# First expert weights loaded behind the last q and k tile, and steps 37 to 40 of an expert loop in conditional parts

## The chip, the cores and the metric

The kernel runs on one core of a Trainium2 chip. The metric is device time in microseconds (us), the median of several executions. The core has five engines with an instruction queue each: TensorE (PE: matmuls and transposes, PEld its weight loads), VectorE (DVE), ScalarE (ACT), GpSimd (POOL) and SyncE (SP). Here SP issues the loads of q, k, v and the weights, and POOL issues the writes of x_rows, the gathers and the scatters; all these transfers run on the same 16 DMA engines. Work passes from engine to engine through semaphores; each queue is served in order.

## The reference

Chunk attention first: q, k and v have the shape (8, 8, 576, 64) (batch, heads, sequence, head size), and a chunk of 64 positions attends only to itself.

```python
scores = scale * np.matmul(q_c, k_c.transpose(0, 1, 2, 4, 3))
scores = scores - np.max(scores, axis=-1, keepdims=True)
attn = np.exp(scores)
attn = attn / (np.sum(attn, axis=-1, keepdims=True) + 1e-09)
out = np.matmul(attn, v_c)
```

Its output, as x with 4608 rows (tokens) of 512, goes through a cosine router to one of 8 experts (w1 512 x 1024, w2 1024 x 512, all float32):

```python
logits = xn @ en.T / tau
expert_idx = np.argmax(logits, axis=1)
...
gate_w = probs[np.arange(N), expert_idx]
...
    h = np.maximum(x[mask] @ w1[e], 0.0)
    out[mask] = gate_w[mask, None] * (h @ w2[e])
```

## The kernel before, in words

There are three stages. The order of the work is written out by hand (`manual_schedule`, line 55): each engine executes its instructions in the order of the program.

**Attention** (lines 85 to 286). 36 tiles (`NT`) of 128 rows. The loop at line 259 is a software pipeline over t: in one iteration TensorE transposes the weights of tile t (`turn_a`), q and k of tile t + 3 (`turn_qk`, line 131), takes the logits of t - 2, the scores of t + 2, the transpose of x for t - 1 and the product with v of t (`values`, line 183). `load_qk(t + 7)` (line 266) puts the next q and k loads on SP's queue; four buffers each hold them, so a load waits until the tile four before it has been turned. `load_v` (line 119) issues eight loads for a batch, every 4.5 tiles. `values` writes the finished tile to a DRAM tensor, x_rows, from POOL's queue (line 210), from one of three x buffers. In the iteration t = 12 (`NT // 3`, line 278) `load_first(0)` (line 73) puts four weight transfers on SP's queue: w1 and w2 of expert 0 and of expert 7, 2 MB each, for the expert loop's first step.

**Seam** (lines 288 to 482). The buffers of attention are released, `late_p` takes part of the room, and `load_first(1)` (line 292) loads the same four weights into the second set. VectorE then works out the routing: the expert of each token, its rank, the gate, and the place of each token in blocks of 64 (`G`) of one expert. Two blocks make a step: side 0 takes the blocks from the front, side 1 from the back, and `mid` (line 382) is half of the number of blocks, rounded. There are tables for up to 40 steps (`NST` = 36 + 4): `src_row` and `dst_row` (which rows to gather and scatter; a row number out of range is left out), `gate_at`, `eblk` (expert of each side and step), `fresh` (1 where the expert differs from that of two steps before, whose buffer is used again).

**Expert loop** (lines 488 to 633). Step j gathers 128 rows (`gather`, four buffers ahead), transposes them (`turn_xb`), multiplies with w1 (`hidden`: 32 matmuls of 512 columns, the two sides on the two halves of the output partitions, then ReLU on VectorE and ScalarE), transposes h (`turn_h`), multiplies with w2 (`result`: 32 matmuls) and scatters the rows (line 598). The loop at line 619 is a software pipeline too: its body holds `hidden(j + 1)`, `turn_h(j)`, `turn_xb(j + 2)`, `result(j - 1)`, so that each copy out of PSUM has matmuls of another step beside it. `load_w1` and `load_w2` read expert and `fresh` into registers of SP (line 499) and issue a 2 MB transfer that takes place only where `fresh` is 1; it waits for the matmuls that read the buffer last. All 40 steps are issued.

Of the kernel before, what the change touches and what calls it, by code (L numbers as in the profile page):

```python
# [9 lines left out]
FP32 = mybir.dt.float32  # L10
BF16 = mybir.dt.bfloat16
I32 = mybir.dt.int32
AF = mybir.ActivationFunctionType
ALU = mybir.AluOpType
AX = mybir.AxisListType
PSUM = bass.MemoryType.PSUM
ENG = mybir.EngineType

P = 128
# [6 lines left out]
def kernel(  # L26
# [11 lines left out]
    nc = tc.nc  # L38
    B, H, S, Dh = q.shape
    E, D = moe_expert_emb.shape  # L40
    F = moe_w1.shape[2]
    N = B * S
    NPAIR = H // 2
    KD = D // P
    KF = F // P
    NT = N // P
    NCB = S // CH
    G = P // 2
    NST = NT + E // 2
# [4 lines left out]
    keep = ctx.enter_context(tc.tile_pool(name="keep", bufs=1))  # L54
    ctx.enter_context(tc.manual_schedule())


    w1_sb = [[keep.tile([P, KD, F], FP32, name=f"w1_{s}0")] for s in range(2)]
    w2_sb = [[keep.tile([P, KF, D], FP32, name=f"w2_{s}0")] for s in range(2)]
    w1_rows = moe_w1.rearrange("e (c p) f -> p (e c) f", p=P)  # L60
    w2_rows = moe_w2.rearrange("e (c p) d -> p (e c) d", p=P)
# [5 lines left out]
    gate_at = keep.tile([P, NST], FP32, name="gate_at")  # L67
    eblk = keep.tile([1, 2, NST], I32, name="eblk")
    fresh = keep.tile([1, 2, NST], I32, name="fresh")

    make_identity(nc, ident)

    def load_first(i):

        for s in range(2):
            e = (0, E - 1)[s]
            nc.sync.dma_start(out=w1_sb[s][i], in_=w1_rows[:, e * KD : e * KD + KD, :])
        for s in range(2):
            e = (0, E - 1)[s]
            nc.sync.dma_start(out=w2_sb[s][i], in_=w2_rows[:, e * KF : e * KF + KF, :])  # L80

# [2 lines left out]
    with (  # L86
# [18 lines left out]
        def load_qk(t):  # L105
            for src, nm in ((k, "kx"), (q, "qx")):
                x = qk_p.tile([P, H, Dh], FP32, tag=nm, name=nm)
                done = 0
                while done < P:
                    b, s = divmod(t * P + done, S)  # L110
                    n = min(P - done, S - s)
                    nc.sync.dma_start(  # L112
                        out=x[done : done + n],
                        in_=src[b, :, s : s + n, :].rearrange("h p d -> p h d"),
                    )
                    done += n
                qk_t[nm, t] = x.rearrange("p h d -> p (h d)")
# [13 lines left out]
        def turn_qk(t):  # L131
            for nm in ("kx", "qx"):
                a = qk_t.pop((nm, t))
                ps = ps_t.tile([P, NPAIR, P], FP32, tag="tr", name="tr")
                for i in range(NPAIR):
                    nc.tensor.transpose(ps[:, i], a[:, i * P : i * P + P], ident)  # L136
                x = wk.tile([P, NPAIR, P], FP32, tag=nm + "T", name=nm + "T")
                if nm == "kx":
                    nc.scalar.copy(x, ps)
                else:  # L140
                    nc.vector.tensor_copy(x, ps)  # L141
                qkT[nm, t] = x
# [31 lines left out]
        def turn_a(t):  # L174
            d = st[t]
            ps = ps_t.tile([P, NPAIR, P], FP32, tag="tr", name="tr")
            for i in range(NPAIR):
                nc.tensor.transpose(ps[:, i], d["a"][:, i].rearrange("p r k -> p (r k)"), ident)  # L178
            aT = wk.tile([P, NPAIR, P], FP32, tag="aT", name="aT")
            nc.scalar.copy(aT, ps)  # L180
            d["aT"] = aT
# [77 lines left out]
        for t in range(-3, NT + 2):  # L259

            if 0 <= t < NT:
                turn_a(t)
            if t + 3 < NT:
                turn_qk(t + 3)
                if t + 7 < NT:
                    load_qk(t + 7)
            if 0 <= t - 2:
                logits(t - 2)
            if 0 <= t + 2 < NT:
                scores(t + 2)  # L270
            if 0 <= t - 1 < NT:
                turn_x(t - 1)
            if 0 <= t < NT:
                values(t)
                b = (2 * t + 2) // NCB + 1
                if b not in v_t and b < B:
                    load_v(b)
                if t == NT // 3:
                    load_first(0)
            if 0 <= t + 2 < NT:  # L280
                weights(t + 2)
            if 0 <= t < NT:
                norm(t)
            if t == -2:
                set_up_experts()
        nc.vector.tensor_copy(lg, lg_ps)

    late_p = ctx.enter_context(tc.tile_pool(name="late", bufs=1))
    for s in range(2):
        w1_sb[s].append(late_p.tile([P, KD, F], FP32, name=f"w1_{s}1"))  # L290
        w2_sb[s].append(late_p.tile([P, KF, D], FP32, name=f"w2_{s}1"))
    load_first(1)

# [5 lines left out]
    with (  # L301
# [7 lines left out]
        io = sp.tile([P, P], FP32, name="io")  # L309
# [66 lines left out]
        mid = sp.tile([P, 1], FP32, name="mid")  # L376
# [28 lines left out]
        for i in range(2):  # L405
            nc.vector.tensor_scalar(
                fresh[:, i, 0:2], e_of[:, i, 0:2], float((0, E - 1)[i]), None, ALU.not_equal
            )
        nc.vector.tensor_tensor(
            fresh[:, :, 2:NST], e_of[:, :, 2:NST], e_of[:, :, 0 : NST - 2], ALU.not_equal  # L410
        )


# [12 lines left out]
            out=row, in0=blk, scalar=-float(G), in1=dest, op0=ALU.mult, op1=ALU.add  # L426
# [3 lines left out]
            out=row, in0=back, scalar=float(G), in1=row, op0=ALU.mult, op1=ALU.add  # L430
# [32 lines left out]
        for s in range(NT):  # L463
# [17 lines left out]
            out=dst_row, in0=tk, scalar=-1.0, in1=bad, op0=ALU.add, op1=ALU.add  # L481
# [7 lines left out]
    with (  # L489
# [5 lines left out]
    ):  # L495
        xin, mo = {}, {}

        def number(ap, top, engine):
            return nc.values_load(
                ap,  # L500
                engines=(engine,),
                min_val=0,
                max_val=top,
                skip_runtime_bounds_check_because="a count of comparisons, less than this",
            )
# [22 lines left out]
        def gather(j):  # L528
            t = bp.tile([P, D], FP32, tag="xin", name="xin", bufs=XBUF)
            nc.gpsimd.indirect_dma_start(  # L530
                out=t,
                out_offset=None,
                in_=x_rows,
                in_offset=bass.IndirectOffsetOnAxis(ap=src_row[:, j : j + 1], axis=0),
                bounds_check=N - 1,
                oob_is_err=False,
            )
            xin[j] = t
# [77 lines left out]
        hidden(0)  # L616
        load_w1(2)
        turn_xb(1)
        for j in range(NST + 1):
            if j + 1 < NST:  # L620
                hidden(j + 1)
                if j + 3 < NST:
                    load_w1(j + 3)
            if j < NST:
                turn_h(j)
            if j + 2 < NST:
                turn_xb(j + 2)
            if j > 0:
                result(j - 1)
                if j + 1 < NST:  # L630
                    load_w2(j + 1)
            if j + XBUF < NST:
                gather(j + XBUF)


# [26 lines left out]
```

## Time and profile before

| | |
|---|---|
| median of 3 runs (lowest to highest) | 862.99 us (862.68 to 863.69) |
| the profiled execution, its own time | 861.98 us |
| its span, first to last instruction | 860.2 us |
| mean granted TensorE clock | 0.956 |
| busy: PE / PEld / DVE / ACT / POOL | 794.9 / 392.8 / 223.8 / 187.4 / 105.2 us |
| moved by DMA | 142.58 MB, mean 166 GB/s |

A time of an engine in a row is its busy time; "L136" is line 136 of the kernel. A stretch A:B runs from A to B us after the span's start. The granted clock (PEclk) is a share of TensorE's full 2.4 GHz; 0.50 is its lower level, 1.2 GHz. A share of busy time is an average over stages with different limits, so each stage is read for itself.

### The profile page before, as it was taken

The page shows a single profiled execution, that of the slowest core. Times are in us where ns is not written, and L with a number is a line of the kernel's source. Part 1 is how long each engine was busy: PE and PEld are TensorE (multiplying, and loading weights), DVE is VectorE, ACT ScalarE, POOL GpSimd, SP SyncE. Part 2 cuts the span into 40 slices and gives each one's busy share as a digit, 9 for nine tenths or more (in the row PEclk, how much of TensorE's full clock was granted, in tenths as well). Part 3 has the DMA queues.
Part 4 walks back from the last instruction along what each step waited for, and adds up shares of the span by engine and source line. Part 5 has one row for each costly group of instructions (what it writes and reads, how often), then busy time and mean ns, then how long its engine had stood idle before and what let it go on. Part 6 is the DMA issues. An engine that isn't in the chain of part 4 may idle for free.

```text
span 860.2 us, 15300 instructions
## 1 busy us (share of the span) xinstructions
PE 794.9 (92%) x6287; PEld 392.8 (46%) x6287; DVE 223.8 (26%) x436; ACT 187.4 (22%) x346; POOL 105.2 (12%) x136
## 2 busy tenths in 40 slices
PE   5899299980789999999999999999999999999997
PEld 4799288970733333333333333333333334333332
DVE  3677256758511101011010110101101011010110
ACT  4577246761000111011110111101111111111011
POOL 1111001110110011010110101001010010100101
PEclk9999789995589999999999999999999999999999
DMA  9999999929110001045763157875214252147560
GB/s 208 238 246 274 376 229 245 251 98 348 61 47 22 26 34 41 25 146 192 263 231 123 50 188 272 330 307 196 74 37 151 107 197 74 38 154 298 200 234 1
DMA packets 153670, 142.58 MB, mean 166 GB/s; under 512 B 115702, under 2 KB 115702, under 8 KB 153600
## 3 DMA queue, kind: packets, MB, share of 16 engines
q1 hardware_dynamic: 144256, 112.21, 42.7%
q0 software_dynamic: 9344, 29.39, 9.6%
q8 instruction: 50, 0.82, 0.4%
q14 instruction: 20, 0.16, 0.1%
HBM read 391.14 MB, written 19.92 MB: 478 GB/s over the span
## 4 chain that ended last, share of the span: by engine, by line
issue 69%; PE 15%; POOL 7%; DMA 4%; DVE 3%; POOLq 0%; ACT 0%; SPq 0%; DVEq 0%; ACTq 0%
POOL xin L530 5%; PE tr L136 3%; PE lg_ps L229 2%; PE sc L152 2%; DMA kx<-in_k_dram 2%; POOL out_dram L598 2%; PE inv L466 2%; PE pv L192 2%; PE tr L178 2%; PE tr L221 2%; DMA qx<-in_q_dram 2%; POOL x_rows L210 1%; DMA x_rows<-x 0%; SPq L112 0%; POOLq L530 0%
## 5 line engine op out<-in xcount | busy, mean ns | idle before, releaser
L556 PE MATMUL h_ps<-w,xbT 128*64 128x512 f32 x1280 | 283.2, 595 | 2.4 <-DVE xbT L546 2.4
L589 PE MATMUL y_ps<-w,hT 128*64 128x512 f32 x1280 | 283.3, 595 | 0.0
L556 PEld LDWEIGHTS h_ps<-w,xbT 128*64 128x64 f32 x1280 | 92.0, 138 | 185.5 <-issue 182.3
L589 PEld LDWEIGHTS y_ps<-w,hT 128*64 128x64 f32 x1280 | 88.4, 137 | 167.0 <-issue 167.0
L567 DVE TENSOR_SCALAR h<-h_ps 128x512 f32<-128x512 f32 x40 | 27.7, 692 | 376.5 <-PE h_ps L556 376.5
L598 POOL DMA_INDIRECT out_dram<-y,dst_row x40 | 40.6, 1014 | 531.2 <-ACT y L597 515.8
L597 ACT ACTIVATE y<-y_ps,gate_at 128x512 f32<-128x512 f32 x40 | 27.5, 688 | 272.6 <-PE y_ps L589 272.6
L565 ACT ACTIVATE h<-h_ps 128x512 f32<-128x512 f32 x40 | 24.0, 600 | 284.0 <-PE h_ps L556 284.0
L581 DVE COPY hT<-ht_ps 128x512 f32<-128x512 f32 x40 | 27.7, 692 | 136.6 <-PE ht_ps L577 136.6
L577 PEld LDWEIGHTS ht_ps<-ident,h 128*128 128x128 f32 x320 | 34.3, 140 | 32.5 <-issue 32.5
L530 POOL DMA_INDIRECT xin<-x_rows,src_row x40 | 41.0, 1024 | 49.5 <-DVE dst_row L480 37.6
L136 PE MATMUL tr<-ident,kx 128*128 128x128 f32 x144 | 24.1, 294 | 22.3 <-DMA kx<-in_k_dram 22.3
L577 PE MATMUL ht_ps<-ident,h 128*128 128x128 f32 x320 | 43.7, 280 | 0.0
L210 POOL DMA_DIRECT2D x_rows<-x x36 | 19.6, 544 | 168.7 <-DVE x L203 140.3
L229 PEld LDWEIGHTS lg_ps<-enT,xT 128*128 128x128 f32 x288 | 35.9, 196 | 1.0 <-ACT xT L223 0.9
L229 PE MATMUL lg_ps<-enT,xT 128*128 128x8 f32 x288 | 35.5, 250 | 0.7 <-ACT xT L223 0.7
L141 DVE COPY qxT<-tr 128x512 f32<-128x512 f32 x36 | 24.9, 692 | 36.1 <-PE tr L136 34.3
L160 DVE TENSOR_REDUCE mx<-sc 128x8 f32<-128x512 f32 x36 | 24.9, 692 | 26.9 <-PE sc L152 26.9
L546 DVE COPY xbT<-x_ps 128x512 f32<-128x512 f32 x40 | 27.7, 692 | 13.8 <-PE x_ps L544 9.3
L544 PE MATMUL x_ps<-ident,xin 128*128 128x128 f32 x160 | 24.5, 277 | 5.2 <-DMA xin<-x_rows,src_row 5.2
L466 PE MATMUL inv<-rr,oh 128*128 128x80 f32 x72 | 15.7, 422 | 14.6 <-DVE oh L465 14.6
L136 PEld LDWEIGHTS tr<-ident,kx 128*128 128x128 f32 x144 | 18.1, 151 | 23.7 <-issue 15.2
(118 smaller groups left out, 503.2 us busy)
## 6 DMA issues: line engine op xcount, KB each, us to landing
w<-in_moe_w_dram SPq DMA_DIRECT2D x168, 2048.0 KB
v<-in_v_dram SPq DMA_DIRECT2D x64, 144.0 KB
x_rows<-x POOLq DMA_DIRECT2D x36, 256.0 KB, 3.7
kx<-in_k_dram SPq DMA_DIRECT2D x32, 256.0 KB
qx<-in_q_dram SPq DMA_DIRECT2D x32, 256.0 KB
kx<-in_k_dram SPq DMA_DIRECT2D x8, 128.0 KB
qx<-in_q_dram SPq DMA_DIRECT2D x8, 128.0 KB
xin<-x_rows,src_row POOLq DMA_INDIRECT x40, 3.6
```

The source lines that it names most:

```text
L136: nc.tensor.transpose(ps[:, i], a[:, i * P : i * P + P], ident)
L210: nc.gpsimd.dma_start(out=x_rows[P * t : P * t + P, :], in_=x)
L229: nc.tensor.matmul(lg_ps[:, t], lhsT=d["xT"][:, c], rhs=enT[:, c], start=(c == 0), stop=(c == KD - 1),)
L466: nc.tensor.matmul(inv.rearrange("p t k -> p (t k)"), lhsT=oh, rhs=rr[:, s].rearrange("p t k -> p (t k)"), start=(s == 0), stop=(s == NT - 1),
L530: nc.gpsimd.indirect_dma_start(out=t, out_offset=None, in_=x_rows, in_offset=bass.IndirectOffsetOnAxis(ap=src_row[:, j : j + 1], axis=0), ...
L546: nc.vector.tensor_copy(xT, ps)
L556: nc.tensor.matmul(ps[G * s : G * s + G], lhsT=d["xT"][:, c, G * s : G * s + G], rhs=w1_sb[s][j % 2][:, c, fh * 512 : fh * 512 + 512], sta ...
L567: nc.vector.tensor_scalar(dst, ps, 0.0, None, ALU.max)
L577: nc.tensor.transpose(ps[:, c], d["h"][:, f0 : f0 + P], ident)
L581: nc.vector.tensor_copy(hT[:, 4 * g : 4 * g + 4], ps)
L589: nc.tensor.matmul(ps[G * s : G * s + G], lhsT=d["hT"][:, c, G * s : G * s + G], rhs=w2_sb[s][j % 2][:, c], start=(c == 0), stop=(c == KF ...
L598: ins = nc.gpsimd.indirect_dma_start(out=out, out_offset=bass.IndirectOffsetOnAxis(ap=dst_row[:, j : j + 1], axis=0), in_=y, in_offset=Non ...
```

## The change

Six of the eight tiles of the first weights (all but the second set of w2) now lie in the pool that lives through the whole kernel. `load_first` loads one matrix of both sides. In the iteration t = 29, where the last `load_qk` has been issued in the iteration before, SP issues six weight transfers (w1 of both sets, w2 of the first); w2 of the second set is still loaded after attention, into `late_p`, which is now half as large. `load_first(0)` at t = 12 is gone.

In the seam, `used` marks the steps below `mid`, `n_steps` keeps `mid` as an integer, and `fresh` is multiplied by `used`.

The expert loop's pipeline runs over 36 steps (`LEAST`). Then all five engines read `n_steps` into a register, and `more(36)` holds step 37 whole, one part after the other, under a condition; inside it is the condition for step 38, and so on to step 40.

```diff
-    w1_sb = [[keep.tile([P, KD, F], FP32, name=f"w1_{s}0")] for s in range(2)]
+    w1_sb = [[keep.tile([P, KD, F], FP32, name=f"w1_{s}{i}") for i in range(2)] for s in range(2)]
...
-    def load_first(i):
+    def load_first(buf, rows, n, i):
 
         for s in range(2):
             e = (0, E - 1)[s]
-            nc.sync.dma_start(out=w1_sb[s][i], in_=w1_rows[:, e * KD : e * KD + KD, :])
-        for s in range(2):
-            e = (0, E - 1)[s]
-            nc.sync.dma_start(out=w2_sb[s][i], in_=w2_rows[:, e * KF : e * KF + KF, :])
+            nc.sync.dma_start(out=buf[s][i], in_=rows[:, e * n : e * n + n, :])
...
                 if t + 7 < NT:
                     load_qk(t + 7)
+                elif t + 7 == NT:
+                    load_first(w1_sb, w1_rows, KD, 0)
+                    load_first(w1_sb, w1_rows, KD, 1)
+                    load_first(w2_sb, w2_rows, KF, 0)
...
-                if t == NT // 3:
-                    load_first(0)
...
     for s in range(2):
-        w1_sb[s].append(late_p.tile([P, KD, F], FP32, name=f"w1_{s}1"))
         w2_sb[s].append(late_p.tile([P, KF, D], FP32, name=f"w2_{s}1"))
-    load_first(1)
+    load_first(w2_sb, w2_rows, KF, 1)
...
+        used = sp.tile([1, NST], I32, name="used")
+        nc.vector.tensor_scalar(used, io[0:1, 0:NST], mid[0:1], None, ALU.is_lt)
+        nc.vector.tensor_copy(n_steps, mid[0:1])
         nc.vector.tensor_tensor(
             fresh[:, :, 2:NST], e_of[:, :, 2:NST], e_of[:, :, 0 : NST - 2], ALU.not_equal
         )
+        nc.vector.tensor_tensor(
+            fresh, fresh, used.unsqueeze(1).to_broadcast([1, 2, NST]), ALU.mult
+        )
...
-        for j in range(NST + 1):
-            if j + 1 < NST:
+
+        LEAST = NT
+        for j in range(LEAST + 1):
+            if j + 1 < LEAST:
                 hidden(j + 1)
                 if j + 3 < NST:
                     load_w1(j + 3)
-            if j < NST:
+            if j < LEAST:
                 turn_h(j)
-            if j + 2 < NST:
+            if j + 2 < LEAST:
                 turn_xb(j + 2)
             if j > 0:
                 result(j - 1)
...
+        steps = number(n_steps, NST, ENG.PE, ENG.DVE, ENG.Activation, ENG.Pool, ENG.SP)
+
+        def more(j):
+            with tc.If(steps > j):
+                turn_xb(j)
+                hidden(j)
+                if j + 2 < NST:
+                    load_w1(j + 2)
+                turn_h(j)
+                result(j)
+                if j + 2 < NST:
+                    load_w2(j + 2)
+                if j + 1 < NST:
+                    more(j + 1)
+
+        more(LEAST)
```

## Rows read from the trace of the kernel before

**Rows 1.** Busy time by stretch: engines, then PEclk, DMA share, GB/s.
```profile
30.00:77.00 47.00, 47.00 (x987) 43.45 (x987) 34.97 (x70) 32.43 (x68) 6.52 (x14) 1.00 1.04 247
91.00:107.00 16.00, 1.92 (x49) 1.40 (x40) 2.35 (x5) 2.41 (x5) 0.54 (x1) 0.62 1.03 375
194.00:237.00 43.00, 16.85 (x79) 16.14 (x79) 29.61 (x95) 3.24 (x4) 3.93 (x7) 0.50 0.54 204
249.00:825.00 576.00, 575.22 (x2854) 217.80 (x2852) 78.86 (x114) 69.84 (x112) 72.44 (x71) 1.00 0.41 146
```

**Rows 2.** Waits of SP's queue, 25 to 77 us: total, times, longest.
```profile
SPq L112 <- PE tr L136: 9.3, 11, 1.8
```

**Rows 3.** Timeline of POOL in attention: start, duration, instruction, idle time before.
```profile
39.96 0.54 POOL L210 DMA_DIRECT2D x_rows<-x  x1 [3.60 <-DVE x L203]
...
89.08 0.54 POOL L210 DMA_DIRECT2D x_rows<-x  x1 [3.55 <-DVE x L203]
94.06 0.54 POOL L210 DMA_DIRECT2D x_rows<-x  x1 [4.44 <-DVE x L203]
115.87 0.54 POOL L210 DMA_DIRECT2D x_rows<-x  x1 [21.27 <-DMA qx<-in_q_dram]
...
182.12 0.54 POOL L210 DMA_DIRECT2D x_rows<-x  x1 [3.55 <-DVE x L203]
```

**Rows 4.** Timeline of SP's issues in attention.
```profile
77.51 2.01 SPq L77 DMA_DIRECT2D w<-in_moe_w_dram  x2
...
90.85 4.26 SPq L112 DMA_DIRECT2D kx<-in_k_dram  x1
...
169.95 0.81 SPq L112 DMA_DIRECT2D qx<-in_q_dram  x1
```

**Rows 5.** Timeline of the seam.
```profile
194.60 0.20 POOL masks.py:65 MEMSET sltb<- 128x128 bf16 x1 [2.06 <-DMA x_rows<-x]
...
204.41 0.22 DVE L409 TENSOR_TENSOR fresh<-e_of 1x76 int32<-1x76 f32 x1
```

**Rows 6.** Timeline of POOL at the end of the expert loop.
```profile
780.87 1.02 POOL L598 DMA_INDIRECT out_dram<-y,dst_row  x1 [13.00 <-ACT y L597]
...
826.90 1.01 POOL L598 DMA_INDIRECT out_dram<-y,dst_row  x1 [14.33 <-ACT y L597]
...
856.74 0.98 POOL L598 DMA_INDIRECT out_dram<-y,dst_row  x1 [5.93 <-ACT y L597]
```

**Rows 7.** The scatters of line 598, 812 to 828 us.
```profile
DMA to landing us min/median/max: 7.0/7.0/7.0
```

**Rows 8.** The scatters of line 598, 850 to 861 us.
```profile
DMA to landing us min/median/max: 2.1/2.1/2.1
```

**Rows 9.** The writes of line 210 (x_rows), 78 to 96 us.
```profile
DMA to landing us min/median/max: 5.5/5.9/6.3
```

**Rows 10.** The writes of line 210 (x_rows), 165 to 195 us.
```profile
DMA to landing us min/median/max: 2.3/3.1/3.7
```

**Rows 11.** Timeline of TensorE at the start of the expert loop.
```profile
238.51 8.68 PE L556 MATMUL h_ps<-w,xbT 128*64 128x512 f32 x32 [0.79 <-DVE xbT L546]
247.13 0.66 PE L544 MATMUL x_ps<-ident,xin 128*128 128x128 f32 x4
248.57 3.65 PE L556 MATMUL h_ps<-w,xbT 128*64 128x512 f32 x16 [0.78 <-DVE xbT L546]
```

**Rows 12.** Timeline of the kernel's last microseconds.
```profile
840.70 1.09 PE L577 MATMUL ht_ps<-ident,h 128*128 128x128 f32 x8
...
841.45 0.69 DVE L581 COPY hT<-ht_ps 128x512 f32<-128x512 f32 x1 [7.35 <-PE ht_ps L577]
...
841.73 13.95 PE L589 MATMUL y_ps<-w,hT 128*64 128x512 f32 x64
```

**Rows 13.** SP's register loads at line 499: duration ns min/median/max, first and last start.
```profile
L499 SPq TENSOR_LOAD <-eblk x80: 262/268/474, 204.4 to 802.2; - x80
```

**Rows 14.** The queue that fetches instructions: packets, MB, share of 16 engines.
```profile
q8 instruction: 50, 0.82, 0.4%
```

More of the change, by code (lines that the diff above doesn't have):

```diff
@@ L69 @@
     fresh = keep.tile([1, 2, NST], I32, name="fresh")
+    n_steps = keep.tile([1, 1], I32, name="n_steps")
     make_identity(nc, ident)
-    def load_first(i):
+    def load_first(buf, rows, n, i):
         for s in range(2):
             e = (0, E - 1)[s]
-            nc.sync.dma_start(out=w1_sb[s][i], in_=w1_rows[:, e * KD : e * KD + KD, :])
-        for s in range(2):
-            e = (0, E - 1)[s]
-            nc.sync.dma_start(out=w2_sb[s][i], in_=w2_rows[:, e * KF : e * KF + KF, :])
+            nc.sync.dma_start(out=buf[s][i], in_=rows[:, e * n : e * n + n, :])
     VW = 72
@@ L496, with number @@
         xin, mo = {}, {}
-        def number(ap, top, engine):
+        def number(ap, top, *engines):
             return nc.values_load(
                 ap,
-                engines=(engine,),
+                engines=engines,
                 min_val=0,
```

## The prediction

> **What bounds the kernel now.** I read the busy times by stretch first, then the issues of POOL and SP in order of time through attention, then the timelines of the seam, of the expert loop and of its end, and last the landings. They show three stages, and a bound for each.
>
> In attention TensorE is busy for all of 30 to 77 us while the DMA engines move 247 GB/s [rows 1], and in nearly that stretch it is SP that waits for TensorE to free q and k buffers, 11 times at one line alone [rows 2]: TensorE sets the pace, one tile of 128 rows in (89.08 - 39.96) / 12 = 4.09 us [rows 3]. Then the four weight transfers that `load_first(0)` puts on SP's queue (issued from 77.51 us) hold the queue; the next k tile is not issued before 90.85 us [rows 4]. In 91 to 107 us TensorE does 1.92 us of work at a granted clock of 0.62, which mixes 2.4 and 1.2 GHz, while DMA moves 375 GB/s [rows 1]: 8.39 MB of weights stand ahead of 256 KB that TensorE needs. The tile written out at 94.06 is followed by the next at 115.87 [rows 3].
>
> The seam (the routing between attention and the experts) is one long chain on VectorE with transfers beside it; its first work waits for the last write of x_rows [rows 5].
>
> In the expert loop TensorE is busy 575.22 of 576 us at the full clock, 2.4 GHz [rows 1]. A step costs (826.90 - 780.87) / 3 = 15.34 us by the scatters [rows 6]. All 40 steps are paid, whether or not they hold tokens. How many do is fixed by the inputs: the reference's argmax gives the experts 832, 359, 183, 448, 512, 1023, 576 and 675 tokens, in blocks of 64 that is 13, 6, 3, 7, 8, 16, 9 and 11, together 73, two to a step: 37 steps (j = 0 to 36). The trace agrees: the scatter at 826.90 is that of j = 36 (the one at 856.74 is j = 39, two lie between) and took 7.0 us to land [rows 6, 7], the last ones landed in 2.1 us [rows 8].
>
> **The change, attention.** Tiles 16 to 33 (first and last of 17 intervals: 89.08 and 182.12) took 93.04 us, and 17 x 4.09 is 69.6 [rows 3]. The loss around the weights is thus 23.4 us, close to 8.39 MB at 375 GB/s = 22.4 us. Moved behind tile 36's q and k, the weights have no q, k or v load behind them on SP (v for the last batch is issued earlier). Six transfers move, 12.6 MB, about 34 us at that rate: from some 147 us (the last q tile's issue, 169.95 [rows 4], less 23.4) to about 185 us with the x_rows writes among them. I take the whole 23.4 as gained, and give back 0.9: the tile at 94.06 came 4.98 us after the one before instead of 4.09, the loads already on the way having shared the engines with the weights, and the last tile will meet that. Bounds: 0, as its loads are ahead in the queue, and 2 us, if its 512 KB go at half of 375 GB/s beside weights.
>
> **The seam.** The remaining `load_first` (4.2 MB, 11 us) starts when attention's buffers are released and queues behind the flood; no matmul of the loop begins before 238.51 [rows 11], 44 us after that release [rows 5], so it costs nothing. The x_rows writes on POOL's queue do pay. In the present flood four landed in 5.5 to 6.3 us, median 5.9 [rows 9]; the last ones of attention, with little beside them, took as little as 2.3 [rows 10]. Three x buffers cover 6.3 us at a tile each 3.3 us or more. But the last write is what POOL's first seam work waits for [rows 5], and it now falls into the flood (attention ends near 170 us): 5.9 - 2.3 = **+3.6**. Bounds: 0, if the flood thins out or the buffers reused are others, and 4.0. Three small VectorE operations are added (`used`, `n_steps`, the product with `fresh`); the one next to them took 0.22 us [rows 5]: **+0.6**, bounds 0.3 and 0.7. SP's loads of `fresh` come later by that much, which nobody feels, as both first weight sets are there.
>
> **The loop.** Steps 37 to 40 leave the pipelined loop: -4 x 15.34 = **-61.4**. Step 37 then runs by itself in the order turn, hidden, turn, result. A turn of x with its copy exposed shows at the loop's start: 247.13 to 248.57, 1.44 us [rows 11]. `result` is 13.95 / 2 = 6.98 us, and `hidden`, as many matmuls of the same size, too; the turn of h is 0.75 us until the copy begins (840.70 to 841.45) plus 0.69 us of copy, 1.5 with the hand-over [rows 12]. Together **+16.9**. Its second copy hides behind the first half of `result`. Its weights: j = 36 has a fresh expert on one side; the w2 load is issued after `result` of j = 34, and between that and its use lie `result` of j = 35 and the first three of these, 16.9 us for 2.1 MB (5.6 us at 375 GB/s), so that is covered; w1 has longer. Masking `fresh` removes six later loads, whose cover was the same TensorE work: nothing. On SP, the loads of j = 38 wait inside the conditional part for step 37's matmuls, with only its own branch behind them. POOL's gathers stay ahead of the conditional part.
>
> **The end and the branches.** The last scatter now carries rows. It took 2.1 us empty [rows 8], 7.0 beside a weight load [rows 7]; nearest is a quiet write of the same 256 KB, 3.1 [rows 10]: **+1.0**, bounds 0 and 4.9. Reading `n_steps` on five engines and two branches on each: no row shows a branch. A register load took 0.26 to 0.47 us [rows 13]. At the entry I take **+0.5** on TensorE; below 0, since its sequencer may run ahead of the array; above 6.2, if the part begins with all engines joined: from TensorE's last matmul to the end of the span are 860.2 - 855.68 = 4.5 us, and after such a gap `hidden` may run as after the seam, 8.68 instead of 6.98 [rows 11, 12]. A gain is excluded, as only instructions are added. At the exit every engine jumps over three bodies: **+1.1**, what one 16 KB packet of the instruction queue takes (0.4% of 16 x 860.2 us over 50 packets [rows 14]); below 0, hidden behind the scatter's landing; above 6.9, three jumps one after another at the shortest landing of a write, 2.3 for rows written [rows 10].
>
> The Trainium skill's Runtime: NRT & Kernel Launch, section Instruction fetch mechanics, says that a taken branch to code outside the two pages held forces a fetch before execution goes on. No run here shows that yet. By it alone the exit would be one fetch or more, by a free branch 0.
>
> **The sum.** -23.4 + 0.9 + 3.6 + 0.6 - 61.4 + 16.9 + 1.0 + 0.5 + 1.1 = -60.2 against the profiled execution's 861.98 us (span 860.2): 801.8. The median of the runs, 862.99, is 1.0 above that execution; so 802.8, **803**.
>
> **Rivals.**
> First, dear branches: three fetches in a row at the exit, 6.9 instead of 1.1, make 803 + 5.8 = 809; a join at the entry, 6.2 instead of 0.5, makes 809 too, and both 815. For it: the conditional part can't mix with work outside it, and five engines read the count each for itself. Against it: only two branches lie on the path, and the exit has a landing to hide behind. The fetches are what the cited page of the Trainium skill would lead one to expect.
>
> Second, attention stays short of data. A tile needs 1.05 MB in 4.09 us, 256 GB/s, and 30 to 77 us shows 247 [rows 1]; if the loads fall behind by that 3.5% over the 20 later tiles, 82 us, that gives 3 us back: 806. Against it: SP waits for buffers in that very stretch [rows 2], so loading is ahead.
>
> Third, the change doesn't skip. If the count read were 40, three more lone steps with their entries would run, 3 x (16.9 + 0.5) = 52: 855. Against it: the count of 37 above.
>
> Fourth, on the other side: the clock. In the seam TensorE is granted 1.2 GHz (0.50 [rows 1]), and it has 2.4 GHz back within the first `hidden` (8.68 against 6.98 us [rows 11, 12]). If that came later by more than the 60 us saved, the kernel would be slower: four steps at half speed cost 61. At eight steps it would be 803 + 8 x 15.34 = 926. Against it: the same work stands there as before.
>
> **How the numbers follow.** The forecast has 0.64 and holds 796 to 807: its low end leaves out the 0.9, the 3.6, the 1.0 and the 1.6 of branches (803 - 7.1 = 796), its high end adds 4 us of the bounds. Dear branches have 0.20 (0.10 the fetches, 0.07 the join, 0.03 both), attention short of data 0.12, no skip 0.03, the clock 0.01. The range is 796 to 812: it takes in the second rival and the cases with one dear branch, and leaves out two of them together, no skip and the clock. A measurement of this kernel tells 0.2%, 1.7 us, from no change. All cases but the last are faster by more than that; I leave 0.01 for no change, since several terms could fail at once.
>
> **What would show it.** In the profile of the changed kernel: x_rows written every 4.09 us from the fourth tile to the 33rd without a gap; weight issues only after the last q tile; landings near 6 us at attention's end and the seam's first POOL work released by one; 37 scatters, the last with TensorE gaps under 1 us before its `hidden` and its `result`. Gaps of 4 us and more there, or a long stretch after the last matmul, would mean dear branches; waits for kx after 90 us, the second rival; 40 scatters, the third; a loop step over 15.34 us, the fourth. Outside 796 to 812 a term of the sum is wrong.

## The result and the profile after

The changed kernel takes 820.47 us (818.87 to 823.09, 4 runs); the kernel before, run beside it, 863.34 us (862.68 to 864.77). The ratio is 0.9504, 95% interval 0.9476 to 0.9533. The change saves 43 us where 60 were forecast, and 820 is outside the range of 796 to 812. The profiled execution took 820.02 us, its span 818.2 us against 860.2: -42.0.

Attention first. This is POOL's timeline of the changed kernel (start, duration, instruction, idle time before), which answers to [rows 3, 5].

```profile
43.67 0.54 POOL L208 DMA_DIRECT2D x_rows<-x  x1 [3.61 <-DVE x L201]
...
117.44 0.54 POOL L208 DMA_DIRECT2D x_rows<-x  x1 [3.55 <-DVE x L201]
127.56 0.54 POOL L208 DMA_DIRECT2D x_rows<-x  x1 [9.57 <-DVE x L201]
133.21 0.54 POOL L208 DMA_DIRECT2D x_rows<-x  x1 [4.94 <-DVE x L201]
...
179.90 0.54 POOL L208 DMA_DIRECT2D x_rows<-x  x1 [2.75 <-DVE x L201]
186.94 0.20 POOL masks.py:65 MEMSET sltb<- 128x128 bf16 x1 [6.50 <-DMA w<-in_moe_w_dram]
...
225.88 1.10 POOL L535 DMA_INDIRECT xin<-x_rows,src_row  x1 [38.07 <-DVE dst_row L485]
```

The 21.8 us gap behind the tile of 94.06 [rows 3] is gone. But the fourth tile comes at 43.67 instead of 39.96, 3.7 late before any moved instruction is reached, and there is a new gap: 117.44 to 133.21 holds two intervals of 10.12 and 5.65 us instead of 4.09, 7.6 lost. So the last write moves from 192.00 to 179.90, 12.1 us, where 22.5 were forecast. From it to the seam's first POOL work it is 7.04 us, before 194.60 - 192.00 = 2.60; the profile names a weight transfer as releaser, but the last write of x_rows took 6.3 us to land, which is about the same moment (the landings of the last six writes):

```profile
DMA to landing us min/median/max: 5.9/6.3/7.5
```

The windows of the changed kernel, the columns as in [rows 1] (the last two numbers are the DMA share and GB/s, ahead of them the granted clock):

```profile
30.00:77.00 47.00, 47.00 (x980) 42.90 (x983) 34.23 (x67) 30.93 (x65) 6.29 (x13) 0.97 1.02 233
91.00:107.00 16.00, 16.00 (x332) 14.64 (x332) 11.79 (x24) 11.13 (x25) 2.32 (x5) 1.00 1.09 236
242.00:780.00 538.00, 537.22 (x2664) 203.09 (x2662) 72.63 (x105) 65.41 (x105) 69.15 (x68) 1.00 0.37 131
```

TensorE now works through 91 to 107 us, and in the expert loop it is busy 537.22 of 538 us at the full clock. But the same loads arrive at 233 GB/s in 30 to 77 us, where it was 247. That stretch alone tells little: f1 below has 234 GB/s there and is faster.

Last, the end of the changed kernel, by TensorE's timeline [rows 12] and then POOL's [rows 6]:

```profile
773.20 13.95 PE L594 MATMUL y_ps<-w,hT 128*64 128x512 f32 x64
787.09 0.66 PE L549 MATMUL x_ps<-ident,xin 128*128 128x128 f32 x4
788.53 7.09 PE L561 MATMUL h_ps<-w,xbT 128*64 128x512 f32 x32 [0.78 <-DVE xbT L551]
795.54 1.45 PE L582 MATMUL ht_ps<-ident,h 128*128 128x128 f32 x8
797.04 7.09 PE L594 MATMUL y_ps<-w,hT 128*64 128x512 f32 x32
```

```profile
805.22 1.00 POOL L603 DMA_INDIRECT out_dram<-y,dst_row  x1 [15.96 <-ACTq L645]
```

The lone step 37 takes 804.13 - 787.09 = 17.0 us, the parts as reckoned, and it begins right behind the step before: TensorE loses nothing at the entry to the conditional part. But from the last matmul (804.13) to the end of the span are 14.07 us, where it was 4.5. The stretches add up (us of the profiled executions):

| stretch | forecast | measured |
|---|---|---|
| last write of x_rows | -22.5 | -12.1 |
| from it to the seam's first work | +3.6 | +4.4 |
| seam to the first gather (38.47, now 38.94) | +0.6 | +0.5 |
| first gather to last matmul (622.61, now 578.25) | -44.0 | -44.4 |
| last matmul to the end | +2.1 | +9.55 |
| sum | -60.2 | -42.0 |

Two terms are wrong, attention by 10.4 us and the end by 7.45.

### The profile page after: what moved, and what is told of

It is laid out like the page before. It is cut to its first block, busy times and chain, and to the rows that moved or that the text cites. A ratio compares the mean times of both kernels' runs of the same rounds, so it can differ in the third digit from the quotient of the medians.

```text
span 818.2 us, 14809 instructions
## 1 busy us (share of the span) xinstructions
PE 749.4 (92%) x6059; PEld 375.7 (46%) x6059; DVE 217.9 (27%) x430; ACT 181.6 (22%) x337; POOL 101.9 (12%) x133
## 2 busy tenths in 40 slices
DMA packets 148726, 129.99 MB, mean 159 GB/s; under 512 B 115366, under 2 KB 115366, under 8 KB 148656
## 3 DMA queue, kind: packets, MB, share of 16 engines
q1 hardware_dynamic: 139552, 99.63, 42.5%
## 4 chain that ended last, share of the span: by engine, by line
PE 86%; DMA 6%; DVE 3%; issue 2%; SPq 1%; ACT 1%; POOL 0%; POOLq 0%
PE y_ps L594 31%; PE h_ps L561 30%; PE ht_ps L582 5%; PE tr L134 4%; DMA w<-in_moe_w_dram 3%; PE lg_ps L227 3%; PE sc L150 3%; PE pv L190 2%; PE tr L176 2%; PE tr L219 2%; DMA qx<-in_q_dram 2%; PE x_ps L549 2%; PE inv L471 2%; DMA xin<-x_rows,src_row 0%; SPq L78 0%
## 5 line engine op out<-in xcount | busy, mean ns | idle before, releaser
L561 PE MATMUL h_ps<-w,xbT 128*64 128x512 f32 x1184 | 262.2, 595 | 3.1 <-DVE xbT L551 3.1
L594 PE MATMUL y_ps<-w,hT 128*64 128x512 f32 x1184 | 262.0, 595 | 0.0
L561 PEld LDWEIGHTS h_ps<-w,xbT 128*64 128x64 f32 x1184 | 85.0, 138 | 172.3 <-issue 168.0
L594 PEld LDWEIGHTS y_ps<-w,hT 128*64 128x64 f32 x1184 | 81.8, 137 | 154.6 <-issue 154.3
L572 DVE TENSOR_SCALAR h<-h_ps 128x512 f32<-128x512 f32 x37 | 25.6, 692 | 341.0 <-PE h_ps L561 341.0
L603 POOL DMA_INDIRECT out_dram<-y,dst_row x37 | 37.5, 1013 | 490.1 <-ACT y L602 474.1
L602 ACT ACTIVATE y<-y_ps,gate_at 128x512 f32<-128x512 f32 x37 | 25.4, 688 | 251.8 <-PE y_ps L594 245.2
L582 PEld LDWEIGHTS ht_ps<-ident,h 128*128 128x128 f32 x296 | 31.7, 141 | 30.4 <-issue 30.0
L582 PE MATMUL ht_ps<-ident,h 128*128 128x128 f32 x296 | 40.7, 280 | 0.1
L134 PE MATMUL tr<-ident,kx 128*128 128x128 f32 x144 | 24.6, 299 | 10.8 <-DMA kx<-in_k_dram 10.7
L213 ACT ACTIVATE junk<-x 128x512 f32<-128x512 f32 x36 | 22.7, 630 | 21.9 <-DVE x L201 21.9
```

Of the source, the lines that this page charges most:

```text
L561: nc.tensor.matmul(ps[G * s : G * s + G], lhsT=d["xT"][:, c, G * s : G * s + G], rhs=w1_sb[s][j % 2][:, c, fh * 512 : fh * 512 + 512], sta ...
L572: nc.vector.tensor_scalar(dst, ps, 0.0, None, ALU.max)
L582: nc.tensor.transpose(ps[:, c], d["h"][:, f0 : f0 + P], ident)
L594: nc.tensor.matmul(ps[G * s : G * s + G], lhsT=d["hT"][:, c, G * s : G * s + G], rhs=w2_sb[s][j % 2][:, c], start=(c == 0), stop=(c == KF ...
L603: ins = nc.gpsimd.indirect_dma_start(out=out, out_offset=bass.IndirectOffsetOnAxis(ap=dst_row[:, j : j + 1], axis=0), in_=y, in_offset=Non ...
```

## The experiments

The theories, by letter where an expectation uses one. **A**: attention falls short of data, since a tile needs 256 GB/s and gets less (the second rival of the prediction). **B**: the end is long because of the conditional parts. **C**, formed after the first four runs: the 4-byte tile `n_steps` moves all later buffers by 32 bytes, and that slows the loads. **D**, also formed then: POOL needs the time at the end behind a scatter that writes rows, with or without conditional parts. **E**: the seam's late start comes from the weight flood alone. The kernel before took 865.72 us beside e1 to e4, 866.0 beside f1 to f4 and 865.95 beside g1 to g4.

**e1_again.** The changed kernel, no edit.

> The changed kernel, unaltered, profiled once more. Theory A (the loads of q, k and v together with the x_rows writes need 256 GB/s and the DMA engines give about 237): TensorE again waits for q and k in mid-attention, 5 to 10 us in all after the third tile, and the last x_rows write is issued at 176 to 183 us. Rival (the wait of 6 us before the tile written at 127.56 was a chance of that execution): no wait over 2 us after the third tile, last write at 168 to 173 us. The end after the last matmul again takes 13 to 15 us by every theory.

One run took 825.26 us (span 823.5). The last x_rows write came at 184.63, just outside the 176 to 183 of A, and the end was 14 us again. Attention's stalls vary by some 5 us between executions; the rest repeats.

**e2_weights_only.** The kernel before with the part of the change in `w1_sb`, `load_first`, its calls and `late_p`; no `n_steps`, no conditional parts.

> The weight loads moved, the loop as before with all 40 steps. Theory A: attention 10 to 14 us shorter than before, the seam's start 4 us later after the last x_rows write: 863.3 - 12.1 + 4.4 = 855.6 us (853 to 859). The prediction's reckoning (the whole 23.4 us are gained) would give 863.3 - 22.5 + 3.6 = 844.4 us.

846.89 us (845.99 to 849.78), ratio 0.9788 (0.9758 to 0.9817). That is nearer to the prediction's reckoning than to A. POOL's timeline of this run:

```profile
37.82 0.54 POOL L207 DMA_DIRECT2D x_rows<-x  x1 [3.61 <-DVE x L200]
...
95.13 0.54 POOL L207 DMA_DIRECT2D x_rows<-x  x1 [3.55 <-DVE x L200]
103.28 0.54 POOL L207 DMA_DIRECT2D x_rows<-x  x1 [7.21 <-DVE x L200]
109.11 0.54 POOL L207 DMA_DIRECT2D x_rows<-x  x1 [5.28 <-DVE x L200]
...
172.19 0.54 POOL L207 DMA_DIRECT2D x_rows<-x  x1 [2.75 <-DVE x L200]
179.09 0.20 POOL masks.py:65 MEMSET sltb<- 128x128 bf16 x1 [6.36 <-DMA w<-in_moe_w_dram]
```

Moving the weights alone brings the last write to 172.19, 19.8 us earlier. The gap is there, as A says, but the late start of the fourth tile is not. Something in the other half of the change slows attention.

**e3_cond_only.** The changed kernel without e2's part: weights loaded as before, conditional parts kept.

> The conditional parts alone, the weights loaded as before. Theory B (the end pays some 9.5 us more because POOL has to make up for skipped scatters): 863.3 - 44.4 + 0.6 + 9.5 = 829 us (827 to 831), 14 us from the last matmul to the end of the span. If the end were cheap without the moved weights: 820 us.

844.05 us (842.91 to 845.58), ratio 0.9746 (0.972 to 0.9771): 15 us more than expected, and not at the end (843.3 - 829.2 = 14.1 us behind the last matmul, as in the changed kernel) but in attention, where this edit moves no instruction. The last write comes at 207.19 instead of 192.00. Already the first 20 us show it (window of this run):

```profile
0.00:20.00 20.00, 10.06 (x97) 7.93 (x98) 5.47 (x12) 7.05 (x10) 2.28 (x10) 1.00 1.21 190
```

190 GB/s, where the kernel before moves 209 with the same instructions. What differs there is where the buffers lie. `n_steps` stands in the pool `keep` behind `fresh`; it takes 32 bytes of each partition, and all later buffers follow it. In the memory plan of the built programs (not of a trace) kx begins at byte 84992 before (332 x 256), at 85024 in e3 (32 more) and at 117792 in the changed kernel (460 x 256 + 32, behind two more w1 tiles). This is C.

**e4_static37.** The changed kernel with 37 steps in the loop and no conditional parts (37 is what these inputs need).

```diff
-        LEAST = NT
+        LEAST = NT + 1
...
-        steps = number(n_steps, NST, ENG.PE, ENG.DVE, ENG.Activation, ENG.Pool, ENG.SP)
...
-        more(LEAST)
```

> The changed kernel with a plain loop of 37 steps and no conditional part (right for these inputs only, since the count is not asked). It gives the whole price of the branches: theory B 820.5 - 9.1 at the end - 1.6 for the lone step = 809.8 us (808 to 812), 5 us from the last matmul to the end. If the long end came from somewhere else (the last scatter with rows, or the gathers of steps that do not run), it stays at 13 to 15 us and the time is 819 us.

824.93 us (820.27 to 829.44), ratio 0.9545 (0.9511 to 0.9579), its interval overlaps that of the changed kernel. Its last matmuls in TensorE's timeline, and POOL's DRAIN at the end (by line: count, duration ns min/median/max, first and last start):

```profile
799.10 7.08 PE L594 MATMUL y_ps<-w,hT 128*64 128x512 f32 x30 [2.68 <-DMA w<-in_moe_w_dram]
```

```profile
L664 POOLq DRAIN  x3: 51/99/10707, 807.0 to 818.2; - x3
```

The end is 818.5 - 806.18 = 12.3 us long without any branch, so B can hold for 14.07 - 12.3 = 1.75 us only. Most of it is one DRAIN of POOL, 10.7 us. In the plain loop TensorE also waits 2.68 us for the last w2, which the lone step hides.

**f1_pad.** The changed kernel, `n_steps` in a tile of 256 bytes, so that later buffers move by 256 instead of 32.

```diff
-    n_steps = keep.tile([1, 1], I32, name="n_steps")
+    n_steps = keep.tile([1, 64], I32, name="n_steps")[:, 0:1]
```

> The changed kernel with n_steps given 256 bytes a partition in place of 4, so that the buffers behind it (q, k, v, x and those of the loop) start where they start in the kernel before, at a multiple of 256 bytes, and not 32 bytes behind one. Theory C (the 32 bytes cost the 256-byte packets of q and k their speed): the first 20 us move 205 to 215 GB/s as in the kernel before and not 188, the last x_rows write comes at 171 to 174 us and not at 180 to 185, the time falls by 8 to 10 us: 811 to 815. Rival (the place in memory does not matter, the DMA engines were only slower in those executions): 188 GB/s again, time as the changed kernel's, 820 to 825.

**f2_before_shift.** The other way round: the kernel before with an unused 4-byte tile.

```diff
     fresh = keep.tile([1, 2, NST], I32, name="fresh")
+    shift = keep.tile([1, 1], I32, name="shift")
+    nc.vector.memset(shift, 0)
```

> The kernel before with one unused tile of 4 bytes a partition behind fresh, nothing else: every later buffer moves by 32 bytes. Theory C: 187 to 190 GB/s in the first 20 us, the last x_rows write at 203 to 208 us (207.2 in the run with the conditional parts alone) and not at 192, time 863 + 13 = 876 us (872 to 879). Rival: 862 to 867 us, no difference.

f1: 814.27 us (812.24 to 814.35), ratio 0.9393 (0.9358 to 0.9428), below the changed kernel's interval. f2: 875.11 us (874.85 to 879.62), slower than the kernel before: ratio 1.012 (1.0076 to 1.0165). The first 20 us of the changed kernel and of f1 (windows):

```profile
0.00:20.00 20.00, 9.74 (x98) 7.61 (x99) 5.18 (x11) 7.05 (x10) 2.27 (x10) 1.00 1.20 188
```

```profile
0.00:20.00 20.00, 10.07 (x136) 8.10 (x136) 6.69 (x14) 8.03 (x12) 2.27 (x10) 0.83 1.05 209
```

and the queue that carries SP's loads on their pages (packets, MB, share of 16 engines' span), again the changed kernel and f1:

```profile
q1 hardware_dynamic: 139552, 99.63, 42.5%
```

```profile
q1 hardware_dynamic: 139552, 99.63, 40.8%
```

The buffers moved by 32 bytes get 188 GB/s, the others 209, and the DMA share is the higher one (1.20 against 1.05) while less is moved: the packets take longer. The same 139,552 packets take 0.425 x 818.2 - 0.408 x 812.6 = 16.2 us more of all 16 engines. The other pair says the same: f2 moves 188 GB/s in its first 20 us, the kernel before 209, and this queue has 43.9% of f2's span of 873.1 us and 42.7% of 860.2 before, 16.0 us more. C is shown in both directions, and by all 14 profiles: in the first 20 us the five kernels with the shift of 32 bytes move 187 to 190 GB/s, the nine others 204 to 215. Why a packet to a moved buffer takes longer, no run shows. By the last x_rows write, six executions with weights behind attention and unmoved alignment (e2, f1, f3, f4, g1, g3) lie at 171.1 to 174.5, mean 173.0; the three moved by 32 bytes (the changed kernel, e1, e4) at 179.9 to 184.6, mean 181.5.

The Trainium skill (DMA: Bandwidth & Descriptors, How a descriptor splits into AXI transactions) says that where a descriptor doesn't start on a multiple of 256 bytes, its first transaction starts at the multiple below, and the bytes ahead of the start cost although they are unused. The direction agrees: 188 GB/s against 209, and 115,366 of 148,726 packets here are under 512 bytes. The page tells it of reads and gives no time, while here the written side moved; only shifts of 0, 32 and 256 bytes were run.

**f3_static_nogather.** f1 with e4's edit, and no gathers for the steps left out.

```diff
-            if j + XBUF < NST:
+            if j + XBUF < LEAST:
                 gather(j + XBUF)
```

> As f1_pad, but a plain loop of 37 steps without conditional parts, and without the gathers of the steps that do not run (right for these inputs only). Theory D (the long end belongs to the last scatter, which now has rows to write): 11 to 13 us from the last matmul to the end of the span, POOL's drain 9 to 11 us. Rival (the gathers of the unused steps still keep POOL busy at the end): 4 to 6 us, drain 3 us. Time 811 us by D, 804 by the rival.

**f4_no_last_scatter.** f3 without the scatter of step 37; its rows stay unwritten.

```diff
+            if j == NT:
+                return
             ins = nc.gpsimd.indirect_dma_start(
                 out=out,
```

> As f3_static_nogather, with the scatter of step 37 left out, so that its 64 rows are not written and the last scatter is that of step 36, some 8 us earlier. Theory D, if POOL needs about 10 us after any scatter with rows: the drain ends about 11 us after that scatter, 3 to 5 us after the last matmul; time 7 us under f3_static_nogather. If the drain takes its 10 us however long ago the scatter was: 11 to 13 us after the last matmul, no difference.

f3: 815.26 us (one run, 811 expected by D); scatter at 802.49, with it a DRAIN of 10434 ns, and 12.1 us from the last matmul to the end, so the spare gathers are not the cause. f4: 802.94 us (one run). Its last scatter in POOL's timeline, its last matmuls in TensorE's, and POOL's DRAIN:

```profile
790.25 0.98 POOL L605 DMA_INDIRECT out_dram<-y,dst_row  x1 [7.05 <-ACT y L602]
```

```profile
792.18 7.08 PE L594 MATMUL y_ps<-w,hT 128*64 128x512 f32 x30 [2.12 <-DMA w<-in_moe_w_dram]
```

```profile
L666 POOLq DRAIN  x3: 51/99/10352, 790.0 to 800.9; - x3
```

The DRAIN is as long, but it now follows the scatter of step 36, at 790.25, and lies beside the matmuls of step 37; the kernel ends 801.2 - 799.26 = 1.9 us behind its last one. D holds for a kernel's end: POOL's DRAIN is done 10.1 to 10.5 us after the start of the last scatter, where that writes rows (f4, f3, e4). Not the transfer: the last scatter of the changed kernel and of e4 landed in 2.6 us.

**g1_empty_last.** f1 with one more scatter behind the conditional parts, all of its row numbers out of range, as the last three of the kernel before had them.

```diff
+        zero = bp.tile([P, D], FP32, name="zero", bufs=1)
+        nowhere = bp.tile([P, 64], I32, name="nowhere", bufs=1)
+        nc.vector.memset(zero, 0.0)
+        nc.vector.memset(nowhere, int(NO_ROW))
...
         more(LEAST)
+        ins = nc.gpsimd.indirect_dma_start(
+            out=out,
+            out_offset=bass.IndirectOffsetOnAxis(ap=nowhere[:, 0:1], axis=0),
+            in_=zero,
...
```

> f1_pad with one more scatter behind the conditional parts, all of whose rows are out of range, so that the last scatter again writes nothing, as in the kernel before. Theory D (POOL stays busy for some 10 us after a scatter with rows, whatever follows it): the span ends 12 to 16 us after the last matmul, time as f1_pad, 814 us, or up to 2 us more. Rival (the drain is short whenever the last transfer on POOL's queue writes nothing): 6 to 9 us after the last matmul, 807 us.

809.74 us (808.72 to 812.43), ratio 0.9354 (0.9328 to 0.9379). The end of POOL's timeline in this run, and its DRAIN:

```profile
800.80 1.00 POOL L607 DMA_INDIRECT out_dram<-y,dst_row  x1 [15.96 <-ACTq L649]
807.01 1.00 POOL L662 DMA_INDIRECT out_dram<-zero,nowhere  x1 [5.21 <-issue]
```

```profile
L695 POOLq DRAIN  x3: 51/105/2681, 806.8 to 810.4; - x3
```

The DRAIN is short again, but the empty scatter starts only 6.2 us after the one with rows; the span ends 10.9 us after the last matmul (799.71), 3.2 less than in f1 and between the two expectations: neither theory of this run holds as it was put. Nor is POOL taken up for 10 us by every scatter with rows. In the loop of the changed kernel a gather follows one at once:

```profile
773.29 1.01 POOL L603 DMA_INDIRECT out_dram<-y,dst_row  x1 [12.56 <-ACT y L602]
774.61 1.02 POOL L535 DMA_INDIRECT xin<-x_rows,src_row  x1 [0.31 <-issue]
```

So the 10 us show at the DRAIN, in part at the scatter of this run, and not in the loop; what POOL does in them, no row says.

**g2_late8.** f1 with all eight weight tiles in `late_p`, loaded when attention's buffers are released.

```diff
-    w1_sb = [[keep.tile([P, KD, F], FP32, name=f"w1_{s}{i}") for i in range(2)] for s in range(2)]
-    w2_sb = [[keep.tile([P, KF, D], FP32, name=f"w2_{s}0")] for s in range(2)]
+    w1_sb = [[] for s in range(2)]
+    w2_sb = [[] for s in range(2)]
...
+            w1_sb[s].append(late_p.tile([P, KD, F], FP32, name=f"w1_{s}{i}"))
...
```

> f1_pad with all eight first weight transfers behind attention, into the room that its buffers leave. Theory E (the seam starts late because the last x_rows write lands slowly beside the weights): POOL's first seam work 2.5 to 3 us after the last x_rows write and not 7, and no wait for q and k near the end; the 16.8 MB end near 222 us, at the first gathers, and cost at most 1 us there; time 814.3 - 4.4 = 810 us (808 to 812). Rival (the seam waits for the release of the buffers and the weights do not matter): still 7 us, 814 us, or more if the first step waits for weights.

810.95 us (808.7 to 812.81), ratio 0.9379 (0.9349 to 0.9409). POOL's timeline of this run:

```profile
170.73 0.54 POOL L208 DMA_DIRECT2D x_rows<-x  x1 [2.75 <-DVE x L201]
171.26 0.22 POOL masks.py:65 MEMSET sltb<- 128x128 bf16 x1
...
212.02 1.11 POOL L536 DMA_INDIRECT xin<-x_rows,src_row  x1 [39.87 <-issue]
```

The last write of this run (170.73) landed in

```profile
DMA to landing us min/median/max: 2.3/2.3/2.3
```

against 6.3 beside the weights in the changed kernel, so E is right on the landing. But the seam's first POOL work starts 0.5 us behind the write (7.0 in f1, 180.99 - 173.96), before it has landed and sooner than the 2.5 to 3 us of E: it no longer waits for that write. In the memory plan of the built program the seam's tiles now lie where attention had nothing, so what this run saves is not shown to come from the weights alone. From the last write to the first gather it is 41.3 us (46.0 in f1), 4.7 less; from there to the last matmul 580.8 (578.5), 2.3 more.

**g3_v_aligned.** f1 with the rows of v padded, so that they lie 512 bytes apart. **g4_both.** g2 with the same.

```diff
-VW = 72
+VW = 128
```

> f1_pad with rows of v 512 bytes apart in place of 288, so that the 256-byte packets of v too start at multiples of 256 bytes. Theory C: more than 209 GB/s in the first 20 us, the waits for q and k, 10 us in f1_pad, fall to 2 to 6, time 808 to 811 us. Rival (only q and k matter, or the spacing does not): 209 GB/s, 10 us of waits, 814 us.

> g2_late8 and g3_v_aligned together. If both theories hold: 814.3 - 4.4 - 4 = 806 us (803 to 808). If only the one of the weights: 810. If neither: 814.

g3: 811.49 us (808.82 to 813.5), ratio 0.9376 (0.9342 to 0.941); it moves 213 GB/s in the first 20 us, as e2 does without the padding, and the waits for q and k did not fall as expected (7.3 + 2.8 us, f1 7.0 + 3.2). g4: 809.51 us (808.92 to 811.63), ratio 0.9353 (0.9328 to 0.9377), and not the 806 of both theories together. The intervals of both ratios overlap those of f1, g1 and g2, so what the padding of v is worth is not shown. All four beat the changed kernel and the one before; g4 has the lowest median.

## Why the prediction was wrong

**Most of the views were read rightly.** Attention at 4.09 us a tile, the hold of the weights on SP's queue, a full TensorE in the loop and 37 steps of work all stand; the 23.4 us do not (below). In the changed kernel's trace 37 scatters are issued, and TensorE has no gap of 1 us or more in step 37.

**The step that failed most: "I take the whole 23.4 as gained".** Its bounds went from 0 to 2 us off. The six kernels with unmoved alignment fell short of the predicted last write (192.00 - 22.5 = 169.5) by 173.0 - 169.5 = 3.5 us; the changed kernel's profile by another 6.9.

The kernel before showed part of this. Of the 23.4 us, which the prediction put down to the weights, 2.8 stand in one interval further on (POOL's timeline of the kernel before, then its windows):

```profile
134.07 0.54 POOL L210 DMA_DIRECT2D x_rows<-x  x1 [3.55 <-DVE x L203]
140.97 0.54 POOL L210 DMA_DIRECT2D x_rows<-x  x1 [6.36 <-DVE x L203]
```

```profile
133.00:135.00 2.00, 0.90 (x7) 0.72 (x8) 0.69 (x1) 1.48 (x5) 0.54 (x1) 1.00 1.15 257
137.00:139.00 2.00, 2.00 (x44) 1.55 (x40) 1.38 (x2) 0.65 (x2) 0.00 (x0) 0.50 1.02 232
```

TensorE stood still for 1.1 us and then ran at half the clock, as the changed kernel does behind 117 us. Whether the weights set off this stall too is not shown; without it 20.6 us were to be gained.

The 3.5 is the second rival: the loads fall behind, as its 256 against 247 GB/s said. That its 3 us come so near is in part luck. In the six kernels the fourth tile comes 1.0 us earlier than before (38.9 against 39.96, in the mean), and behind it 4.5 to 6.5 us are lost, of which the profile names 0.9 to 3.6 as waits for q and k. The argument against the rival, that SP waits for buffers, was true of 30 to 77 us, but a buffer that is free early doesn't help a queue whose transfers are slower than their use. In the changed kernel the rate in 40 to 120 us is 230 to 242 GB/s, and the four buffers run out at 117 us. What the wait then costs is more than the wait itself. Windows of the changed kernel:

```profile
116.00:118.00 2.00, 0.31 (x3) 0.07 (x1) 1.02 (x4) 1.39 (x4) 0.54 (x1) 1.00 1.01 221
118.00:120.00 2.00, 1.08 (x4) 0.71 (x4) 0.00 (x0) 0.62 (x2) 0.00 (x0) 0.65 1.05 271
122.00:124.00 2.00, 2.00 (x37) 1.86 (x38) 0.09 (x2) 0.00 (x0) 0.00 (x0) 0.50 0.90 188
126.00:128.00 2.00, 2.00 (x10) 2.00 (x11) 1.06 (x3) 0.73 (x4) 0.44 (x1) 0.50 1.23 239
```

TensorE's waits for q and k in the changed kernel, 100 to 135 us (total, times, longest):

```profile
PE tr L134 <- DMA kx<-in_k_dram: 2.4, 1, 2.4
PE tr L134 <- DMA qx<-in_q_dram: 0.4, 1, 0.4
```

TensorE waited 2.8 us for data. Behind it the granted clock was 0.50, 1.2 GHz, until past 128 us, with TensorE busy nearly all the time, and 7.6 us were lost in all. The other 4.8 are matmuls at half speed. In f1 the stalls are milder: 120.99 - 114.58 and 160.00 - 154.18 instead of 4.09.

The 6.9 (8.5 in the mean of the three executions with the shift) is the 32-byte shift, which the prediction did not see at all. About half of the 8.5 is there by the fourth tile (43.3 against 38.9, in the mean), the rest are longer stalls. It costed `n_steps` as a VectorE operation and not as a tile that moves others. The loads already ran at 247 GB/s for a need of 256, so any loss of rate lands on the path.

**The second failed step: the end, "+1.0" and "+1.1".** The landing itself is about right: 2.1 us empty, 2.6 with rows, +0.5 (step 37 has one block, so the scatter moves 64 rows, 0.13 MB, and not the 256 KB reckoned). But POOL's work after it is not a landing, and the kernel before hides it. POOL's DRAIN in the kernel before, then in the changed one:

```profile
L657 POOLq DRAIN  x3: 51/99/2765, 856.5 to 859.9; - x3
```

```profile
L681 POOLq DRAIN  x3: 51/99/9458, 808.0 to 818.0; - x3
```

Before, 33 us and three empty scatters stand between the last scatter with rows (826.90 [rows 6]) and the end. Now the scatter of step 37 is last, and POOL takes 12.2 us from its start (805.22) to the DRAIN's end (808.0 + 9.5). e4 puts 12.3 - 4.5 = 7.8 us on the scatter, forecast +1.0. The conditional parts add the last 1.75, forecast +1.1: near in size, but for another reason. The line of the condition on POOL's queue in the changed kernel:

```profile
L645 POOLq COMPARE_BRANCH  x3: 38/40/50, 788.6 to 807.8; - x3
...
L645 POOLq INC_SWDGE_SEM  x1: 2511/2511/2511, 805.3 to 805.3; - x1
```

POOL spends 2.5 us in one instruction (INC_SWDGE_SEM) that the kernels without conditional parts don't have at the end, and the DRAIN behind it is 1.2 us shorter than in e4.

**Dear branches, the first rival, came in part and cost nothing.** The compare-and-branch on POOL takes 38 to 50 ns. On TensorE's queue the one at the entry takes 92 ns and the one at the exit, over the three bodies left out, 3442 ns (the line of the condition in windows around 783 and 801 us):

```profile
L645 PEldq COMPARE_BRANCH  x1: 92/92/92, 783.4 to 783.4; - x1
...
L645 PEldq COMPARE_BRANCH  x1: 3442/3442/3442, 799.7 to 799.7; - x1
```

The matmuls queued ahead of it run until 804.13 and cover it. The instruction queue, which moved 50 packets in 818 us, moved three of them in 797 to 804.5 us:

```profile
q8 instruction: 3, 0.05, 3.0%
```

One lies within the branch (799.7 to 803.1), one behind it. In all eight profiles with conditional parts this branch takes 3.3 to 3.9 us; in e4 and f3, without them, the queue moves no packet after 796 us. The fetch that the Trainium skill expects of a taken branch to code outside the two pages held (Runtime: NRT & Kernel Launch, Instruction fetch mechanics) thus agrees with what TensorE's queue shows. The prediction's lower bound, "hidden", is what happened, though behind matmuls and not behind the scatter's landing.

**Right within a microsecond**: the loop (-44.4 for -44.0), step 37 by itself (17.0 for 16.9, with its w2 there in time), the seam's three operations (+0.5 for +0.6), and the last landing in the flood (6.3 for 5.9). The third and fourth rivals did not come: 37 scatters, and the first `hidden` of the loop takes 8.71 us, before 8.68.

## What to carry to other kernels

A new tile, however small, is costed by what it moves: where small packets load the buffers behind it, keep their start on the old alignment, or put the tile last. Where loads run just below the rate that TensorE needs, price a shortage as the wait plus the time at the lower clock behind it, and before a whole excess is put down to one cause, look at the intervals in which it stands. What trails the last scatter of a queue (here POOL's 10 us) counts as soon as nothing is left behind it, so look for empty work at the end of the kernel before that hides it.

## What the runs showed of the hardware that was not expected

- A shift of 32 bytes in the place of the buffers that small packets are loaded into cuts the loads from 209 to 188 GB/s in the first 20 us; a shift of 256 bytes does not.
- POOL's DRAIN at the end takes 9.5 to 10.7 us when the last scatter writes rows (of 128 or 64 alike) and 2.7 to 2.8 when it writes none. In the loop a gather starts 0.3 us behind such a scatter. What POOL does in the DRAIN stays open.
- At the exit from the conditional parts, with three scatters left out, POOL spends 2.5 us in INC_SWDGE_SEM; its branches take 38 to 50 ns.
- TensorE's jump over the three bodies left out takes 3.3 to 3.9 us, with a 16 KB packet of the instruction queue within it; the branch at the entry takes 0.09 us. Matmuls queued ahead hide the jump.
